# A fused attention and MLP kernel on one core: the channel MLP's first product by seven block products

## Chip, core and metric

The kernel runs on one core of a Trainium2 chip. TensorE multiplies, VectorE (DVE), ScalarE (ACT) and GpSimd (POOL) work on tiles in SBUF and PSUM, and SyncE (SP) issues the DMAs. The metric is the device time of one execution in microseconds.

## What is computed

Four batches of 768 tokens with 8 heads of 48 channels go through a decayed linear attention, and the result (384 channels) through two MLP blocks. The second has a mixing over tokens and one over channels:

```python
# first block: x is the attention's output
xn = (x - mu) / np.sqrt(var + 1e-06) * g_ln
x = x + np.maximum(xn @ w_ch1, 0.0) @ w_ch2           # 384 -> 1536 -> 384
# second block
xt = x.transpose(0, 2, 1)
h = np.maximum(xt @ w_tok1, 0.0) @ w_tok2             # 768 -> 256 -> 768
u = x + h.transpose(0, 2, 1)
h2 = np.maximum(u @ w_ch1, 0.0) @ w_ch2               # 384 -> 1536 -> 384
return u + h2
```

The weights reach the core as pairs of 32-bit integers (the halves of a double).

## The kernel before

Every product is made of three matmuls with operands split in a high and a low part: high by high, high by low, low by high. A weight piece of 128 x 384 is loaded (`sg`, 384 KB), turned into floats by three integer steps on VectorE (`convert`, tile `cu`), and split: the high part by a copy on ScalarE, the low part by a subtraction.

Block 1 does attention, normalization and the first MLP in eight steps of 384 tokens, `m0` to `m7`. In it 32 pieces of the weights of block 2 are converted too (`store`, one every 3.8 units of the schedule): the floats go to HBM (`f_d`), whole and not split. `S7` is the start of the last step, `MP2` that of block 2. In block 1 ScalarE writes the high part of each hidden tile (`hh`), VectorE the low part (`hl`), and only with the latter the PSUM bank comes free; there are three such banks (`mm`).

In the last step of block 1 and the start of block 2, `fetch` loads the 32 pieces again (`wf`, 192 KB) and splits them. The token mixing (`tokmix`) of a batch makes `rt` (the six products `rr`, two banks), its high and low part `rh` and `rl`, the products `hh` (`ht`, six tiles), the sum `uu`, and turns each tile by three transposes (`tp`). The channel MLP (`mlp4`) goes over six tiles of 512 tokens: 12 hidden blocks with 9 matmuls of 512 columns each (`mm1`, tile `mm`), ScalarE's relu, VectorE's `hl`, and output tiles `mo` with 36 matmuls of 384 columns (`mm2`), whose result VectorE adds to `xr` (`fin2`) before the store.

`check` runs beside all this in block 2: for each of the 56 weight pieces a load of 384 KB (`cs`), a square on ScalarE, a comparison on VectorE, a subtraction on POOL and a sum on ScalarE. These are called range steps below; they end in one flag (`okt`).

What sets the order: each engine works in order. Every piece of work has a slot number (`Slots`), one unit being 9 matmuls; the emission is sorted by it, and the first 77 units by a table. SP issues its DMAs in that order as well, and an issue that waits holds back those behind it.

Of the kernel before, what the change touches and what calls it, by code (L numbers as in the profile page):

```python
# [21 lines left out]
C = 128  # L22
# [21 lines left out]
P = dict(A=[7, 10, 16, 22, 30, 38, 46, 54, 62], M0=29, LEAD=7, WS=9, WD=2.2, CS=0.5, JQ=42, JD=3.8, JL=6, CKS=6, CKD=2.45,  # L44
         CHK=148, NV=12, WARM0=56, SG=5, PL=4, J=77)
# [95 lines left out]
@with_exitstack  # L141
def fused_kernel(ctx, tc, q_t, k_t, f_t, v_n, v_t, g_rep, w1, w2, wt1, wt2, w3, w4, out):
    nc = tc.nc
    w1, w2, wt1, wt2, w3, w4 = (w.bitcast(I32) for w in (w1, w2, wt1, wt2, w3, w4))
    w1, w2, w3, w4 = (w.rearrange("p (f c) -> p f c", f=FT) for w in (w1, w2, w3, w4))
    x1_d = tc.dram_tile([NU, C, DM], F32, name="x1_d")
    f_d = tc.dram_tile([32, 128, DM], F32, name="f_d")
    with ExitStack() as main:
        flag = main_path(main, tc, q_t, k_t, f_t, v_n, g_rep, w1, w2, wt1, wt2, w3, w4, out, x1_d, f_d)
    general_path(tc, flag, q_t, k_t, f_t, v_t, g_rep, w1, w2, wt1, wt2, w3, w4, out)  # L150
# [7 lines left out]
def main_path(ctx, tc, q_t, k_t, f_t, v_n, g_rep, w1, w2, wt1, wt2, w3, w4, out, x1_d, f_d):  # L158
# [4 lines left out]
    ap = ctx.enter_context(tc.tile_pool(name="ap", bufs=1))  # L163
    xp = ctx.enter_context(tc.tile_pool(name="xp", bufs=9))
    mmp = ctx.enter_context(tc.tile_pool(name="mmp", bufs=3, space=PSUM))
    scp = ctx.enter_context(tc.tile_pool(name="scp", bufs=2, space=PSUM))
    atp = ctx.enter_context(tc.tile_pool(name="atp", bufs=3, space=PSUM))

    ident = const.tile([128, 128], F32, name="ident")
    upper = const.tile([128, HC], F32, name="upper")  # L170
    gln = const.tile([128, DM], F32, name="gln")
    seg = const.tile([P2, NP, C], F32, name="seg")
# [8 lines left out]
    w1h = wp.tile([128, FT, KT, 128], F32R, name="w1h")  # L181
    w1l = wp.tile([128, FT, KT, 128], F32R, name="w1l")
    w2h = wp.tile([128, FT, DM], F32R, name="w2h")
    w2l = wp.tile([128, FT, DM], F32R, name="w2l")

    xt = ap.tile([128, 36, 128], F32R, name="xt")
# [13 lines left out]
    def convert(s0, ld, src, dones, name, step=1, place=None):  # L200
# [23 lines left out]
        for f, x in zip(dones, "hl"):  # L224
            sl.e(s0 + 3 * step, lambda f=f: f(t["u"]), name + "." + x)

# [6 lines left out]
    at = ExitStack()  # L233
    sg = at.enter_context(tc.tile_pool(name="sg", bufs=P["SG"]))
# [276 lines left out]
    def stands(step):  # L511


        if step < N1:
            i = 18 * (step % 2)
            return [xt[:, j:j + 9].rearrange("p (k u) c -> p k (u c)", k=KT) for j in (i, i + 9)]
        if step % 2 == 0:
            return [xt[:, j:j + 12].rearrange("p (k u) c -> p k (u c)", k=KT) for j in (0, 12)]
        return [h[:, 24:36].rearrange("p (k u) c -> p k (u c)", k=KT) for h in hid2()]

    both = {}

    def hid2():
        if not both:
            both.update((x, hp.tile([128, 36, 128], F32R, tag=x, name=x)) for x in ("hh", "hl"))
        return both["hh"], both["hl"]
# [73 lines left out]
    def mlp4(j, s0, fin, out):  # L600

        t = {}
        step = N1 + j

        def mm1(f):
            ps = t[f] = mmp.tile([128, 512], F32, tag="mm", name="mm")
            ah, al = aT[step]
            i = 0
            for k in range(KT):
                for w, x in ((w1h, ah), (w1h, al), (w1l, ah)):  # L610
                    nc.tensor.matmul(ps, w[:, f, k, :], x[:, k, :], start=(i == 0), stop=(i == 8))  # L611
                    i += 1

        def hid(f):
            return [h[:, 4 * (f % 6):4 * (f % 6) + 4].rearrange("p u c -> p (u c)") for h in hid2()]

        def mm1_h(f):
            nc.scalar.activation(out=hid(f)[0], in_=t[f], func=AF.Relu)  # L618

        def mm1_l(f):  # L620
            hh, hl = hid(f)
            nc.vector.scalar_tensor_tensor(hl, t[f], 0.0, hh.bitcast(F32), op0=ALU.max, op1=ALU.subtract)  # L622

        def mm2(u, g):
            if g % 2 == 0:
                t["o", u] = mmp.tile([128, 512], F32, tag="mm", name="mo")
            ps = t["o", u][:, :DM]
            lo, hi = 6 * (g // 2), 6 * (g // 2) + 5
            for f in range(3 * g, 3 * g + 3):
                a, al = (x[:, 128 * u:128 * u + 128] for x in hid(f))  # L630
                for x, w, i in ((a, w2h, 0), (a, w2l, 1), (al, w2h, 2)):
                    nc.tensor.matmul(ps, x, w[:, f, :], start=(f == lo and i == 0), stop=(f == hi and i == 2))  # L632

        for half in range(2):
            for i in range(6):
                f, q = 6 * half + i, s0 + 14 * half + i
                sl.p(q, lambda f=f: mm1(f))
                sl.e(q + 1, lambda f=f: mm1_h(f))
                sl.late(q + 1, lambda f=f: mm1_l(f))
            for u in range(4):  # L640
                for g in (2 * half, 2 * half + 1):
                    q = s0 + 14 * half + 6 + 2 * u + g % 2
                    sl.p(q, lambda u=u, g=g: mm2(u, g))
                sl.late(q + 1, lambda u=u: fin(u, t["o", u][:, :DM]))
                if half:
                    sl.late(q + 1, lambda u=u: out(u))

# [10 lines left out]

    def fin2(j):
        def f(u, ps):  # L660
            x = us[divmod(4 * j + u, NCH)]
            nc.vector.tensor_tensor(x, ps, x, op=ALU.add)  # L662

        def d(u):
            b, s = divmod(4 * j + u, NCH)
            nc.sync.dma_start(out=out[b, 128 * s:128 * s + 128, :], in_=us.pop((b, s)))
        return f, d

# [21 lines left out]

    def store(i, s0, src, key):

        def out(u):
            kept[key] = f_d[len(kept)]
            nc.sync.dma_start(out=kept[key], in_=u)
        convert(s0, s0 - P["JL"], src, (out,), f"s{i}")

# [30 lines left out]
    jobs = [(w[:, 768 * i:768 * i + 768], (k, i)) for i in range(4) for w, k in ((wt1, "t1"), (wt2, "t2"))]  # L728
    jobs += [(w[:, f], (k, f)) for w, k in ((w3, "w3"), (w4, "w4")) for f in range(FT)]
# [387 lines left out]
```

## Time and profile before

| | |
|---|---|
| median of three runs | 780.83 us (779.58 to 781.37) |
| the profiled execution | 780.75 us |
| its span in the trace | 779.0 us |
| TensorE busy | 768.1 us, 99% |
| VectorE, ScalarE, POOL busy | 408.8, 328.1, 179.8 us |
| granted TensorE clock | 0.998 of full |

Busy shares say which engine works; the chain followed back from the last instruction says which work set the end. An instruction's duration in the trace is longer than its distance from the next of its kind, since matmuls overlap.

### The profile page before, as it was taken

The page shows a single profiled execution, that of the slowest core. Times are in us where ns is not written, and L with a number is a line of the kernel's source. Part 1 is how long each engine was busy: PE and PEld are TensorE (multiplying, and loading weights), DVE is VectorE, ACT ScalarE, POOL GpSimd, SP SyncE. Part 2 cuts the span into 40 slices and gives each one's busy share as a digit, 9 for nine tenths or more (in the row PEclk, how much of TensorE's full clock was granted, in tenths as well). Part 3 has the DMA queues.
Part 4 walks back from the last instruction along what each step waited for, and adds up shares of the span by engine and source line. Part 5 has one row for each costly group of instructions (what it writes and reads, how often), then busy time and mean ns, then how long its engine had stood idle before and what let it go on. Part 6 is the DMA issues. An engine that isn't in the chain of part 4 may idle for free.

```text
span 779.0 us, 16825 instructions
## 1 busy us (share of the span) xinstructions
PE 768.1 (99%) x6966; PEld 719.6 (92%) x6966; DVE 408.8 (52%) x805; ACT 328.1 (42%) x841; POOL 179.8 (23%) x177
## 2 busy tenths in 40 slices
PE   8899999999999999999999999999999999999997
PEld 7789999999999999999999899899899899899886
DVE  7898886575656746454352534434434444334421
ACT  6775463343444434442342534434434434334210
POOL 1344121144224442220023441112011111112000
PEclk9999999999999999999999999999999999999999
DMA  9675252445346453442333633225323343323001
GB/s 268 184 227 162 88 161 76 148 131 162 115 129 179 142 167 108 134 138 66 124 99 112 203 82 96 88 81 158 92 76 102 101 142 88 96 82 113 30 2 45
DMA packets 48613, 93.39 MB, mean 120 GB/s; under 512 B 5520, under 2 KB 26128, under 8 KB 48528
## 3 DMA queue, kind: packets, MB, share of 16 engines
q1 hardware_dynamic: 48528, 92.23, 39.3%
q8 instruction: 56, 0.92, 0.5%
q14 instruction: 29, 0.24, 0.1%
HBM read 76.48 MB, written 15.73 MB: 118 GB/s over the span
## 4 chain that ended last, share of the span: by engine, by line
PE 96%; DMA 2%; DVE 1%; SPq 1%; ACT 0%; issue 0%
PE mo L584 20%; PE mm L554 20%; PE mo L632 19%; PE mm L611 19%; PE rt L793 3%; PE ht L817 3%; PE tp L507 2%; PE yT L393 2%; PE yT L384 2%; DMA first<-in_q_t 2%; PE sc L335 1%; PE sc L347 1%; PE y L436 1%; PE kp L312 1%; SPq L257 0%; PE yT L501 0%
## 5 line engine op out<-in xcount | busy, mean ns | idle before, releaser
L554 PE MATMUL mm<-xt,w1h 128*128 128x384 f32 x576 | 150.4, 342 | 0.0
L554 PEld LDWEIGHTS mm<-xt,w1h 128*128 128x128 f32 x576 | 101.7, 188 | 1.7 <-DVE hl L573 0.2
L584 PE MATMUL mo<-w2h,hh 128*128 128x384 f32 x288 | 101.2, 352 | 0.0
L622 DVE SCALAR_TENSOR_TENSOR hl<-mm,hh 128x512 fp32r<-128x512 f32 x72 | 49.8, 691 | 95.4 <-ACT hh L618 95.4
L870 POOL TENSOR_TENSOR cs<-cs 128x384 f32<-128x384 f32 x56 | 46.5, 831 | 227.0 <-DVE cs L867 166.8
L632 PE MATMUL mo<-w2h,hh 128*128 128x384 f32 x288 | 97.5, 339 | 0.0
L584 PE MATMUL mo<-w2h,hl 128*128 128x384 f32 x288 | 96.6, 335 | 0.0
L554 PE MATMUL mm<-xt,w1l 128*128 128x384 f32 x288 | 96.5, 335 | 0.0
L632 PE MATMUL mo<-w2h,hl 128*128 128x384 f32 x288 | 96.5, 335 | 0.0
L584 PE MATMUL mo<-w2l,hh 128*128 128x384 f32 x288 | 96.4, 335 | 0.0
L632 PE MATMUL mo<-w2l,hh 128*128 128x384 f32 x288 | 96.3, 335 | 0.0
L618 ACT ACTIVATE hh<-mm 128x512 fp32r<-128x512 f32 x72 | 43.1, 598 | 124.9 <-PE mm L611 124.9
L569 ACT ACTIVATE hh<-mm 128x384 fp32r<-128x384 f32 x96 | 46.7, 488 | 85.2 <-PE mm L554 85.1
L573 DVE SCALAR_TENSOR_TENSOR hl<-mm,hh 128x384 fp32r<-128x384 f32 x96 | 52.4, 552 | 40.2 <-ACT hh L569 39.9
L611 PE MATMUL mm<-xt,w1h 128*128 128x512 f32 x216 | 67.2, 392 | 0.0
L662 DVE TENSOR_TENSOR xr<-mo,xr 128x384 f32<-128x384 f32 x48 | 26.7, 556 | 73.1 <-PE mo L632 73.1
L584 PEld LDWEIGHTS mo<-w2h,hh 128*128 128x128 f32 x288 | 54.1, 188 | 1.7
L632 PEld LDWEIGHTS mo<-w2h,hh 128*128 128x128 f32 x288 | 54.1, 188 | 0.5
L632 PEld LDWEIGHTS mo<-w2l,hh 128*128 128x128 f32 x288 | 54.1, 188 | 0.4
L584 PEld LDWEIGHTS mo<-w2l,hh 128*128 128x128 f32 x288 | 54.2, 188 | 0.0
L554 PEld LDWEIGHTS mm<-xt,w1l 128*128 128x128 f32 x288 | 54.1, 188 | 0.0
L632 PEld LDWEIGHTS mo<-w2h,hl 128*128 128x128 f32 x288 | 54.1, 188 | 0.0
(162 smaller groups left out, 1486.9 us busy)
## 6 DMA issues: line engine op xcount, KB each, us to landing
cs<-in_w SPq DMA_DIRECT2D x48, 384.0 KB, 3.2
sg<-in_w SPq DMA_DIRECT2D x44, 384.0 KB, 4.6
f_d<-cu SPq DMA_DIRECT2D x32, 192.0 KB, 2.8
wf<-f_d SPq DMA_DIRECT2D x32, 192.0 KB, 2.6
F<-in_f_t SPq DMA_DIRECT2D x21, 224.0 KB, 3.2
T<-in_k_t SPq DMA_DIRECT2D x21, 224.0 KB, 3.1
T<-in_q_t SPq DMA_DIRECT2D x21, 224.0 KB, 4.0
x_d<-x SPq DMA_DIRECT2D x24, 192.0 KB, 2.0
```

Source lines behind the costliest of these rows:

```text
L554: nc.tensor.matmul(ps, w[:, f, k, :], x[:, k, :], start=(i == 0), stop=(i == 8))
L569: nc.scalar.activation(out=hid(f)[0], in_=t[f], func=AF.Relu)
L573: nc.vector.scalar_tensor_tensor(hl, t[f], 0.0, hh.bitcast(F32), op0=ALU.max, op1=ALU.subtract)
L584: nc.tensor.matmul(ps, x, w[:, f, :], start=(f == lo and i == 0), stop=(f == hi and i == 2))
L611: nc.tensor.matmul(ps, w[:, f, k, :], x[:, k, :], start=(i == 0), stop=(i == 8))
L618: nc.scalar.activation(out=hid(f)[0], in_=t[f], func=AF.Relu)
L622: nc.vector.scalar_tensor_tensor(hl, t[f], 0.0, hh.bitcast(F32), op0=ALU.max, op1=ALU.subtract)
L632: nc.tensor.matmul(ps, x, w[:, f, :], start=(f == lo and i == 0), stop=(f == hi and i == 2))
L662: nc.vector.tensor_tensor(x, ps, x, op=ALU.add)
L793: nc.tensor.matmul(t["r"][j][:, :DM], w[:, s, js], t[x, s], start=(s == 0 and i == 0), stop=(s == NCH - 1 and i == 2))
L817: nc.tensor.matmul(ps[:, :DM], w[:, j, js], x[:, j], start=(i == 0), stop=(i == 5))
L870: nc.gpsimd.tensor_tensor(t["u"], t["u"], t["h"], op=ALU.subtract)
```

## The change

The first product of the channel MLP, u by w_ch1, takes a batch's tokens in two halves (three tiles each, 384 columns), and the hidden channels in two halves as well (block f and block f+6). The sum over 384 channels has three blocks. In `strassen` seven products (1, 2, 6, 7, 5, 3, 4), of 11 block pairs in all, replace 12 block pairs of 384 columns. A group `G(g)`, g = 0 to 5, makes hidden blocks g and g+6 for the 768 tokens. Operands are ten sums of token blocks (`xsh`, `xsl`) and nine sums of weight blocks (`ws`, high in 0 to 8 and low in 9 to 17). Product 1 has a bank of its own (`ex`), the others stand in pairs of banks (`pp`, two pairs). VectorE forms the results of a group by four additions (`add2`, two in `add3`, `add4`), three of them 768 columns wide, ScalarE copies product 1 (`copy1`) and takes the high parts (`hi`); the low parts are a 768-column step each (`lo`), on VectorE or POOL.

The weight sums are formed in block 1: a pair of pieces of w_ch1 needs four 128-column sums on VectorE. All 32 pieces are split there and kept in HBM as two parts (`f_d`, `h_d`, `t_d`). In block 2 they are loaded ready: six loads of 1.18 MB (`weights3`), eight of 0.59 MB (`weights4`), and the token weights by 256 KB for every use (`ts`, two buffers). Token mixing of the next batch stands in the groups: RR 0 within group 0, and so on; it has `rt` in two of the three single banks. `check` starts later and its steps come every 3.2 units instead of 2.45, with two buffers for three.

```diff
-P = dict(A=[7, 10, 16, 22, 30, 38, 46, 54, 62], M0=29, LEAD=7, WS=9, WD=2.2, CS=0.5, JQ=42, JD=3.8, JL=6, CKS=6, CKD=2.45,
-         CHK=148, NV=12, WARM0=56, SG=5, PL=4, J=77)
+P = dict(A=[7, 10, 16, 22, 30, 38, 46, 54, 62], M0=29, LEAD=7, WS=9, WD=2.2, CS=0.5, JQ=42, JD=3.8, JL=6, CKS=16, CKD=3.2, CKL=3.2,
+         CHK=199, NV=12, WARM0=56, SG=5, PL=4, J=77)
...
+        def cut(h, l, x, le=nc.vector):
+            nc.scalar.activation(out=h, in_=x, func=AF.Copy)
+            le.tensor_tensor(l, x, h.bitcast(F32), op=ALU.subtract)
...
+            if i == 0:
+                e.scalar_tensor_tensor(v[:, 0], b[:, 0], -1.0, b[:, 1], op0=ALU.mult, op1=ALU.subtract)
+                e.tensor_tensor(v[:, 2], a[:, 0], b[:, 0], op=ALU.subtract)
+            elif i == 1:
+                e.scalar_tensor_tensor(v[:, 1], v[:, 0], -1.0, a[:, 0], op0=ALU.mult, op1=ALU.subtract)
+                e.tensor_tensor(v[:, 3], a[:, 1], v[:, 1], op=ALU.subtract)
+            elif i == 2:
+                cut(r[:, 4:6], q[:, 4:6], b[:, 1:3])
+            else:
+                cut(r[:, 0:4], q[:, 0:4], v[:, 0:4], nc.gpsimd)
...
+    def load_t(m, s):
+        t = tsp.tile([128, 2, JT, 128], F32R, tag="ts", name="ts")
...
+    for g in range(6):
+        sl.e(S7 + FT + 2 + .5 * g, lambda g=g: weights3(g))
+    for i, f in enumerate((0, 6, 3, 9)):
+        sl.e(MP2 + (10, 11, 16, 18)[i], lambda f=f: weights4(f, 3))
...
+        mix = {1: ((6, 5),), 2: ((7, 6), (8, 7)), 6: ((1, 3),), 7: ((2, 2), (5, 9)), 5: ((0, 0),), 3: ((3, 8), (8, 9)),
+               4: ((4, 4), (5, 1))}
+        place = {2: (26, 0), 6: (26, 1), 7: (75, 0), 5: (75, 1), 3: (34, 1), 4: (34, 0)}
...
+            ops = [(w, x) for i, j in mix[m] for w, x in ((ws[:, g, i], xsh[:, j]), (ws[:, g, i], xsl[:, j]),
+                                                          (ws[:, g, 9 + i], xsh[:, j]))]
...
+            nc.scalar.activation(out=q[:, 1], in_=t.pop((g, 1)), func=AF.Copy)
...
+            nc.vector.tensor_tensor(q[:, 0:3:2], t.pop((g, 26))[:, :, :DM], q[:, 1:2].to_broadcast([128, 2, DM]), op=ALU.add)
...
+            nc.vector.tensor_tensor(u, t[g, 75][:, :, :DM], q[:, 2:3].to_broadcast([128, 2, DM]), op=ALU.add)
+            nc.vector.tensor_tensor(q[:, 1], t.pop((g, 75))[:, 1, :DM], u[:, 0], op=ALU.add)
...
+            nc.vector.tensor_tensor(u, t.pop((g, 34))[:, :, :DM], u, op=ALU.add)
...
+        plan = [(G, 0, [0]), (RR, 1), (G, 1, [2]), (RR, 3), (RR, 4), (G, 2, [5]), (RE, 0), (O, 0, 0, E), (O, 1, 0, E),
+                (O, 0, 0, [2]), (O, 1, 0, [2]), (O, 2, 0, R3), (HH, 0), (HH, 3), (O, 3, 0, R3), (HH, 1), (HH, 4),
+                (O, 4, 0, R3), (HH, 2), (HH, 5), (O, 5, 0, R3),
+                (G, 3), (G, 4), (G, 5), (O, 0, 1, E), (TR, 0), (O, 1, 1, E), (TR, 1),
+                (O, 0, 1, [2]), (O, 1, 1, [2]), (TR, 2), (O, 2, 1, R3), (O, 3, 1, R3), (O, 4, 1, R3), (O, 5, 1, R3)]
...
-    cp = ctx.enter_context(tc.tile_pool(name="cp", bufs=3))
+    cp = ctx.enter_context(tc.tile_pool(name="cp", bufs=2))
```

In the plan O(u, half, groups) is the second product of output tile u, RE the split of `rt`, HH and TR the token mixing's second product and the transposes.

**Place A.** VectorE in step `m3` of block 1, before (`hl` frees a bank of the first MLP, `cu` is a conversion, `xn` the normalization):

```order
L573 SCALAR_TENSOR_TENSOR hl<-mm,hh 128x384
L217 SCALAR_TENSOR_TENSOR cu<-sg,cu 128x384
L454 SCALAR_TENSOR_TENSOR xn<-y,nm,gln 128x384
L573 SCALAR_TENSOR_TENSOR hl<-mm,hh 128x384 x2
L207 TENSOR_SCALAR cu<-sg 128x384
L573 SCALAR_TENSOR_TENSOR hl<-mm,hh 128x384
L212 SCALAR_TENSOR_TENSOR cu<-sg,cu 128x384
L573 SCALAR_TENSOR_TENSOR hl<-mm,hh 128x384
```

The same place after (the `sg` steps of 128 and 256 columns are sums and the subtraction of a pair):

```order
L565 SCALAR_TENSOR_TENSOR hl<-mm,hh 128x384
L213 SCALAR_TENSOR_TENSOR cu<-sg,cu 128x384
L457 SCALAR_TENSOR_TENSOR xn<-y,nm,gln 128x384
L565 SCALAR_TENSOR_TENSOR hl<-mm,hh 128x384
L657 SCALAR_TENSOR_TENSOR sg<-cu 128x128
L658 TENSOR_TENSOR sg<-cu 128x128
L565 SCALAR_TENSOR_TENSOR hl<-mm,hh 128x384
L203 TENSOR_SCALAR cu<-sg 128x384
L660 SCALAR_TENSOR_TENSOR sg<-sg,cu 128x128
L661 TENSOR_TENSOR sg<-cu,sg 128x128
L565 SCALAR_TENSOR_TENSOR hl<-mm,hh 128x384
```

Two sums come ahead of the second `hl` of the former pair, and two more ahead of the next.

**Place B.** VectorE in block 2 before, where the token product `rt` of the third batch is split:

```order
L867 SCALAR_TENSOR_TENSOR cs<-cs 128x384
L622 SCALAR_TENSOR_TENSOR hl<-mm,hh 128x512 x2
L867 SCALAR_TENSOR_TENSOR cs<-cs 128x384
L807 SCALAR_TENSOR_TENSOR rl<-rt,rh 128x384 x2
L622 SCALAR_TENSOR_TENSOR hl<-mm,hh 128x512
```

And after, in group 2 of a batch and at the turn to the second product (`q`, `u` are the additions, `hl` the low parts):

```order
L902 TENSOR_TENSOR q<-mm,q 128x2x384
L907 TENSOR_TENSOR u<-mm,q 128x768
L908 TENSOR_TENSOR q<-mm,u 128x384
L1092 SCALAR_TENSOR_TENSOR cs<-cs 128x384
L912 TENSOR_TENSOR u<-mm,u 128x768
L934 SCALAR_TENSOR_TENSOR hl<-q,hh 128x768
L822 SCALAR_TENSOR_TENSOR rl<-rt,rh 128x384 x2
L934 SCALAR_TENSOR_TENSOR hl<-u,hh 128x768
```

The split `rl` stands behind an addition and a low part of 768 columns each, and the last `hl` behind it.

**Place C.** SP around the start of block 2, before (`wf` are weight pieces, `xr` tokens, `cs` range loads):

```order
L860 DMA cs<-in_w 128x768
L758 DMA wf<-f_d 128x384
L777 DMA xr<-x_d 128x384
L758 DMA wf<-f_d 128x384
L777 DMA xr<-x_d 128x384
L860 DMA cs<-in_w 128x768
L758 DMA wf<-f_d 128x384 x2
```

And after (`ts` are the token weights, `w2h` and `w2l` the second weights):

```order
L792 DMA xr<-x_d 128x384
L767 DMA ts<-t_d 128x512
L792 DMA xr<-x_d 128x384
L767 DMA ts<-t_d 128x512
L777 DMA w2h<-h_d 128x1152
L777 DMA w2l<-h_d 128x1152
L777 DMA w2h<-h_d 128x1152
L777 DMA w2l<-h_d 128x1152
L1085 DMA cs<-in_w 128x768
L777 DMA w2h<-h_d 128x1152
```

The large loads stand behind the token loads of the next batch, and the last of these waits for a buffer that RR 3 of the batch frees; the range load comes behind the first four.

## Rows read from the trace of the kernel before

**Rows 1.** The page: busy time of the engines, and the chain's shares.

```profile
PE 768.1 (99%) x6966; PEld 719.6 (92%) x6966; DVE 408.8 (52%) x805; ACT 328.1 (42%) x841; POOL 179.8 (23%) x177
PE 96%; DMA 2%; DVE 1%; SPq 1%; ACT 0%; issue 0%
```

**Rows 2.** Busy time by stretch: us, engines, clock, DMA share, GB/s.

```profile
118.00:379.00 261.00, 261.00 (x3167) 250.54 (x3167) 147.52 (x302) 104.03 (x263) 72.37 (x57) 1.00 0.41 127
...
430.80:774.00 343.20, 342.59 (x1784) 314.80 (x1782) 139.38 (x249) 131.24 (x353) 59.86 (x69) 1.00 0.32 94
```

**Rows 3.** The chain of work that ended last: start, us, what.

```profile
421.07 0.33 PE tp L507 x3
...
723.67 12.28 PE mm L611 x54
...
760.88 12.52 PE mo L632 x72
```

**Rows 4.** Groups of the page: line, names, shapes, count, busy us, mean ns.

```profile
L632 PE MATMUL mo<-w2h,hh 128*128 128x384 f32 x288 | 97.5, 339 | 0.0
...
L611 PE MATMUL mm<-xt,w1h 128*128 128x512 f32 x216 | 67.2, 392 | 0.0
```

**Rows 5.** TensorE's timeline around three transposes: start, us, engine, line.

```profile
420.90 0.49 PE L507 MATMUL tp<-ident,xr 128*128 128x128 f32 x3
421.15 0.42 PE L584 MATMUL mo<-w2h,hh 128*128 128x384 f32 x1
421.41 0.34 PE L584 MATMUL mo<-w2l,hh 128*128 128x384 f32 x1
```

**Rows 6.** Groups by shape, blocks 1 and 2: durations of VectorE's steps.

```profile
L573 DVE SCALAR_TENSOR_TENSOR hl<-mm,hh 128x384 fp32r<-128x384 f32 x96 | 52.4, 552 | 40.2 <-ACT hh L569 39.9
...
L622 DVE SCALAR_TENSOR_TENSOR hl<-mm,hh 128x512 fp32r<-128x512 f32 x72 | 49.8, 691 | 95.4 <-ACT hh L618 95.4
...
L867 DVE SCALAR_TENSOR_TENSOR cs<-cs 128x384 f32<-128x384 f32 x56 | 31.6, 565 | 0.3 <-issue 0.3
...
L807 DVE SCALAR_TENSOR_TENSOR rl<-rt,rh 128x384 fp32r<-128x384 f32 x6 | 3.1, 551 | 0.5 <-ACT rh L801 0.5
```

**Rows 7.** Timeline of the end: the last matmul, the addition, the store.

```profile
773.05 0.34 PE L632 MATMUL mo<-w2h,hl 128*128 128x384 f32 x1
773.42 0.56 DVE L662 TENSOR_TENSOR xr<-mo,xr 128x384 f32<-128x384 f32 x1 [2.57 <-PE mo L632]
774.01 0.33 SPq L666 DMA_DIRECT2D out<-xr  x1
```

**Rows 8.** Timeline in step m3: VectorE, and TensorE's weight load (PEld).

```profile
159.24 1.00 DVE L573 SCALAR_TENSOR_TENSOR hl<-mm,hh 128x384 fp32r<-128x384 f32 x2
159.84 0.30 PEld L554 LDWEIGHTS mm<-xt,w1h 128*128 128x128 f32 x2 [0.21 <-DVE hl L573]
160.44 0.54 DVE L573 SCALAR_TENSOR_TENSOR hl<-mm,hh 128x384 fp32r<-128x384 f32 x1
...
162.24 0.56 DVE L573 SCALAR_TENSOR_TENSOR hl<-mm,hh 128x384 fp32r<-128x384 f32 x1 [0.79 <-ACT hh L569]
...
163.80 0.56 DVE L573 SCALAR_TENSOR_TENSOR hl<-mm,hh 128x384 fp32r<-128x384 f32 x1 [0.54 <-ACT hh L569]
```

**Rows 9.** DMA issues of the page: names, count, KB each, median us to landing.

```profile
wf<-f_d SPq DMA_DIRECT2D x32, 192.0 KB, 2.6
F<-in_f_t SPq DMA_DIRECT2D x21, 224.0 KB, 3.2
T<-in_k_t SPq DMA_DIRECT2D x21, 224.0 KB, 3.1
```

**Rows 10.** DMA of two stretches with full queues, 11 to 12 and 13 to 15 us.

```profile
DMA packets 189, 0.28 MB, mean 282 GB/s; under 512 B 24, under 2 KB 158, under 8 KB 189
...
DMA packets 310, 0.81 MB, mean 404 GB/s; under 512 B 34, under 2 KB 60, under 8 KB 310
```

More of the change, by code (lines that the diff above doesn't have):

```diff
@@ L511, in stands @@
     def stands(step):
[L514 to L526, printed above, removed]
+        i = 18 * (step % 2)
+        return [xt[:, j:j + 9].rearrange("p (k u) c -> p k (u c)", k=KT) for j in (i, i + 9)]
     def transposed(step, u, ps):
@@ L598, in mlp @@
             sl.late(q + 1, lambda u=u: out(u), f"{m}d{u}")
[L600 to L646, printed above, removed]
     def fin1(step):
@@ new lines, in main_path, with hid2, pair @@
+    exp = ctx.enter_context(tc.tile_pool(name="exp", bufs=1, space=PSUM))
+    xsh = p2.tile([128, 10, 384], F32R, name="xsh")
+    xsl = p2.tile([128, 10, 384], F32R, name="xsl")
+    hids = []
+    def hid2():
+        if not hids:
+            hids.extend(hp.tile([128, 36, 128], F32R, tag=x, name=x).rearrange("p (f u) c -> p f (u c)", f=FT)
+                        for x in ("hh", "hl"))
+        return hids
+    def pair(name):
+        return ppp.tile([128, 2, 512], F32, tag="pp", name=name)
@@ L790, in rr, with lt @@
+            t[s] = x[:, 0], x[:, 1]
+            split(t[s][0], t[s][1], us[b, s], nc.vector)
+        def lt(m, s):
+            t["w", m, s] = load_t(m, s)
+        def rr(s):
+            w0 = t.pop(("w", 0, s))
+            if s == 0 and b:
+                t["r"] = [bank("rt")[:, :DM] for _ in range(JT)]
+            elif s == 0:
+                ps = pair("rt")
+                t["r"] = [ps[:, j, :DM] for j in range(JT)]
             for j in range(JT):
-                js = slice(128 * j, 128 * j + 128)
@@ new lines, in main_path, with xmix, mixed @@
+    QA, QD, QP, QS = 0.32, 0.36, 0.55, 0.13
+    def xmix(T, i, end, free=0):
+        sl.e(end + QS, lambda: T["xc"](i))
+        sl.e(end + QS + .6, lambda: T["xs_s"](i))
+        sl.e(max(end + QS + 1.1, free), lambda: T["xs_p"](i))
+    def mixed(T, s, end):
+        sl.e(end + QS, lambda: T["uu"](s))
+    T0 = tokmix(0)
+    for s in range(NCH):
+        sl.e(S7 + 1 + .4 * s, lambda s=s: T0["ld"](s))
+        sl.e(S7 + 1 + .4 * s, lambda s=s: T0["lt"](0, s))
+        sl.e(S7 + 2.5 + .8 * s, lambda s=s: T0["sp"](s))
+        sl.p(S7 + 4 + .9 * s, lambda s=s: T0["rr"](s))
@@ L853, in check @@
+    end = MP2 + 1
+    for b in range(B):
+        end = double(b, end)
+    cp = ctx.enter_context(tc.tile_pool(name="cp", bufs=2))
     def check(i, s0, src):
@@ L873, in fifth @@
             nc.scalar.activation(out=t["u"], in_=t["u"], func=AF.Abs, accum_out=wlow[:, i:i + 1])
-        for d, f in ((-4, first), (0, second), (1, third), (2, fourth), (4, fifth)):
+        for d, f in ((-P["CKL"], first), (0, second), (.6, third), (1.2, fourth), (2.2, fifth)):
             sl.e(s0 + d, f)
@@ L908, in main_path @@
     sl.e(MP2 + P["CHK"] + 2, ranges_e)
-    sl.run(MP2 + 28 * 6 + 2)
+    sl.run(end + 3)
     flag = nc.values_load(oki[0:1, 0:1], min_val=0, max_val=1)
```

367 lines of the change are left out of this document (266 added, 101 removed).

## The prediction

> **What bounds the kernel now.** I read the engines' busy shares and the chain of work that ended last first. TensorE is busy 99% of the span and is 96% of the chain [rows 1]; the second MLP, where the change acts, holds 343.2 us of which TensorE works 342.59 [rows 2]. So the kernel takes what TensorE's instructions take, one behind the other. An instruction's own duration misleads, since they overlap; the chain gives the pitch. 54 first products of 512 columns took 12.28 us, 227.4 ns each; 72 second products of 384 columns took 12.52 us, 173.9 ns each [rows 3]. VectorE's load is the second thing to read: 147.52 of 261.0 us (57%) in block 1, 139.38 of 343.2 (41%) in block 2 [rows 2]. It has room, but as an average.
>
> **What the change takes from TensorE.** Before, the first product of the second MLP is 648 instructions of 512 columns (the 216 of [rows 4], and four forms of 108): 648 x 227.4 ns = 147.4 us. After, a group is 11 block pairs (seven products, four of them of two pairs), three instructions each, 384 columns wide; six groups per batch, four batches: 6 x 4 x 33 = 792 instructions. Those have the shape of the second product, so 792 x 173.9 ns = 137.7 us. Gain: 9.7 us. Transposes: 24 groups of three become 12 groups of six. The next matmul starts 0.25 us after a group of three began, and its successor 0.26 us later instead of 0.17 [rows 5], so each break costs some 0.09 us beside the transposes; the chain's 0.33 us for such a group [rows 3] says the same. 12 breaks fewer are 1.0 us by that and 0.8 if the breaks cost less behind six; I take 0.8. Second product, token mixing and attention keep their instructions. Against the profiled execution (span 779.0 us, 1.75 us around it, 780.75 in all, 0.08 below the median of 780.83) TensorE alone would give 780.75 - 10.5 = 770.25 us. The rest is what TensorE will now wait for.
>
> **VectorE in a group: tight, mostly covered.** Sums of pairs of banks (768 columns) don't occur before. An addition from PSUM of 512 columns takes 691 ns and of 384 takes 552 [rows 6], 139 ns for 128 more, so by a straight line 768 take 0.97 us (0.70, if wide reads cost only what 512 do, to 1.11, two of 384). A group asks add2 0.97, add3 0.97 + 0.56, add4 0.97, lo 0.97: 4.4 us, with a part of a range step (0.565, one per some 5 us) 5.0, of 33 x 0.174 = 5.74. VectorE reads a finished product some 0.2 us after its slot [rows 7]. With a group's start at 0, product 6 ends at 2.09, so add2 runs from 2.29 to 3.26, and the bank pair is wanted at 3.65; add3 ends at 5.38, wanted at 6.26; add4 runs 5.94 to 6.91, wanted at 7.83. Margins of 0.39, 0.88 and 0.92 us: no stall in the plain case, and one range step in front of add2 uses up the first. TensorE's end is set by it only where VectorE falls behind. I charge nothing here; the price if the cover goes is a rival.
>
> **The turn from the first to the second product (three times).** Behind group 2, VectorE has add4 (`u`), lo (`hl`), then the two splits `rl` of the token product and the last `hl` in a row (place B of the order). The token product's banks come free only with `rl`, and the second output tile needs one. add4 ends at 0.2 + 0.97 = 1.17 us from the end of the group, lo at 2.14, the first rl (0.55 us, [rows 6]) at 2.69; TensorE arrives there after 12 second products, 2.09 us. Wait: 0.6 us at each of two turns, 1.3 us (0 to 2.7, with a range step in between). The turn of the first batch is counted below.
>
> **Block 1: more VectorE work between steps that TensorE waits for.** 26 of the 32 weight pieces get a subtraction of about 0.55 us there, the other six (each the second of a pair) four 128-column sums (0.27 us each on the line above) and a 256-column subtraction (0.42): 14.3 + 9.0 = 23 us, which makes 57% about 66. The place matters: at place A of the order the pair's steps come between the subtractions `hl` that free the banks of the first MLP. Before, the weight load of the product that starts at 159.84 us already waited 0.21 us for `hl`, and VectorE runs on without a gap until 160.98 [rows 8]. In after, 0.55 us come ahead of the next `hl` and 0.55 more ahead of the one behind it; idle gaps of 0.79 and 0.54 us follow [rows 8]. I estimate 0.3 us per pair, 1.7 us for six (0, if the gaps take all; 4.5 at 0.75 each).
>
> **The last step of block 1 and the first batch: loads.** Weights for the token mixing come by 256 KB loads into two buffers. In the last step two of them are issued when their buffer comes free, only 15 matmuls (2.6 us) ahead of their use. 192 KB took 2.6 us and 224 KB 3.1 to 3.2 [rows 9]; I take 2.9, so 0.3 us each, 0.6 (0 to 1.5). In batches 0 to 2 one load (for the RR before the last) has 18 matmuls, 3.13 us, the same way: 0 to 0.3 each, 0.5 in all. The six loads of the first weights (1.18 MB each) are issued from about 31 us into the last step; RR of the next batch needs the token data queued behind them at 55.9 us. With full queues the microsecond from 11 moved 282 GB/s, 158 of its 189 packets under 2 KB; the two from 13 moved 404, with 60 of 310 so small [rows 10]. At 404, 7.08 MB are through at 48.5 us and nothing waits; at 282 they are through at 55.9, the token data with 1.6 us of transfer and 2 of landing at 59.5: 3.6 us. I take 404, since the new loads are of long rows (9216 bytes per partition). The second weights' loads stand on SP behind a token load that waits for the end of RR 3 (place C). From there to the first second product are 45 matmuls, 7.8 us; the four loads wanted are 2.36 MB: 5.8 us at 404 and some 2 us to land, with issues 8.3, so 0.5 us late; at 282 GB/s 3.1. In the same turn a range step stands on ScalarE ahead of `rh` and on VectorE ahead of `rl`; it waits for its own load, behind the weights, so the bank wait that is 0.6 elsewhere becomes about 2.2 us. First batch: 0 + 0.5 + 2.2 = 2.7 us (1 to 8.9).
>
> Row against rule: the stretch from 13 us moved 404 GB/s [rows 10]. The Trainium skill, DMA: Bandwidth & Descriptors, section "Specifications", puts the limit from HBM for one core at about 358 GB/s. The trace exceeds it for two whole microseconds, so I don't use it; by it (an estimate) the second weights would take 6.6 us instead of 5.8 and the sum would rise by 0.8 us.
>
> **End.** The flag's bank and the range steps now close inside the last groups: 0.5 us (0 to 1). The path behind the last product stays: the final addition of 384 columns and its store [rows 7].
>
> **Sum.** 1.3 + 1.7 + 0.6 + 0.5 + 2.7 + 0.5 = 7.3 us of waits against a gain of 10.5: 770.25 + 7.3 = 777.55, say 777.5 us.
>
> **Rivals.**
> (a) Hidden after all: the gaps of block 1 take the added work, the loads run at 404 GB/s, the range step's load lands early, and `rl` costs nothing because wide reads are cheaper than the line. Waits of at most 3 us: 771 to 773, say 772. For it: TensorE had no wait worth naming in block 2 before [rows 2], and the margins in a group are positive. Against it: the turn has a wait by durations that are measured.
> (b) Slower: VectorE falls behind in the groups. It works in order, so one step that waits (a range step or a token split whose load or ScalarE partner is late) or is priced too low delays add2, the pair of product 3 then comes late, and the lag is passed on to the next group, since 5.0 of 5.74 us leave little to recover. It decides from a lag of 0.45 us per group on: 24 x 0.45 = 10.8 us alone take the gain. With 2.5 us of the other terms 770.25 + 10.8 + 2.5 = 783.5. For it: the first margin, 0.39 us, is less than one range step of 0.565 [rows 6], and groups 0 to 2 hold six token splits of about 0.55 us each too. Against it: the plain sum, 4.4 us, leaves 1.3.
> (c) No change: the loads at the start of block 2 run at 310 GB/s, between the rows. The first weights are then through at 53.6 us, the token data at 57.1, 1.2 us late; the second weights take 7.6 + 2.5 us against 7.8, 2.3 us late instead of 0.5: 777.5 + 3.0 = 780.5. At 282 it is 3.6 + 2.6 more, 783.7. For it: stores, token loads and range loads share the queues, and 282 was measured with them full; against it: small packets made that number [rows 10].
>
> **How the numbers follow.** Forecast with its surroundings (775 to 779.3) 0.45, of which 0.03 lie within 0.2% of before; (a) 0.20; (c) 0.15; (b) 0.20. 0.2% of the time is 1.56 us, about what a measurement of this kernel tells from no change: faster is below 779.27, slower above 782.39. Faster 0.42 + 0.20 = 0.62, within 0.18, slower 0.20. The range takes in most of (a) and half of (b): 771.5 to 784.
>
> **What would show it.** The chain must show groups of 33 matmuls with 5.74 us, 792 in all at 173.9 ns; if the pitch is larger the first term falls. TensorE's idle time should stand at the turn behind every third group of the first half, with `rl` as releaser; in block 1 behind `hl` where pairs are summed; around the start of block 2 behind loads. TensorE idle in front of product 3 or 2 in most groups, released by the additions, means (b). Range steps waiting for their loads at the start of block 2, and weights landing over 8 us after their issue, mean (c). No idle time at the turns means (a). A 768-column addition of 1.2 us or more would make the forecast wrong upward; below 0.8 us, downward.

## The result and the profile after

The changed kernel takes 789.38 us (median of 4 runs, 789.25 to 793.19) against 781.1 us of before: 1.0122 of its time, interval 1.0089 to 1.0155. It is slower by 8 to 9 us, and lies 5 us above the range of the prediction. One execution of a later run (928 us, at a granted clock of 0.752) belongs to a slow state and is left out of all comparisons. The profiled execution has 789.25 us and a span of 787.5 us. The page's engine totals and the chain's shares, to be put beside [rows 1]:

```profile
PE 763.5 (97%) x7110; PEld 734.8 (93%) x7110; DVE 525.8 (67%) x969; ACT 367.8 (47%) x899; POOL 195.5 (25%) x175
PE 73%; DVE 8%; DMA 5%; issue 5%; ACT 4%; POOL 2%; SPq 1%; DVEq 0%; POOLq 0%; ACTq 0%
```

TensorE works less, as meant, but it no longer is the whole chain: 27% of it now runs over other engines, DMAs and issues. The stretches that answer to [rows 2] (us, busy time of PE, PEld, DVE, ACT, POOL, clock, DMA share, GB/s):

```profile
118.00:379.00 261.00, 260.41 (x3161) 249.53 (x3154) 178.75 (x357) 120.30 (x300) 82.02 (x63) 1.00 0.50 160
432.00:785.50 353.50, 337.36 (x1928) 330.33 (x1926) 222.57 (x348) 157.88 (x381) 78.53 (x72) 1.00 0.40 127
```

In block 1 VectorE has 31 us more work (23 were forecast), and TensorE loses next to nothing. In block 2 TensorE stands still for 16 of 353.5 us; it was 0.6 of 343.2. The chain's rows that answer to [rows 3] (start, us, what), and VectorE's additions by shape, which answer to [rows 6]:

```profile
485.42 15.10 PE mm L892 x87
...
763.25 18.74 PE mo L945 x108
```

```profile
L912 DVE TENSOR_TENSOR u<-mm,u 128x768 f32<-128x768 f32 x24 | 23.0, 957 | 7.5 <-PE mm L892 6.9
L902 DVE TENSOR_TENSOR q<-mm,q 128x768 f32<-128x768 f32 x24 | 22.9, 955 | 10.2 <-ACT cs L1089 4.8 <-PE mm L892 4.6 <-ACT q L898 0.7
```

The pitch of the new products is 15.10 / 87 = 173.6 ns (173.9 forecast), a 768-column addition 0.955 us (0.97 forecast). What the forecast did not have stands in TensorE's waits from 420 us on (what waited, for what: us, times, longest):

```profile
PE mm L892 <- DVE q L902: 4.1, 5, 2.3
PE rt L812 <- DVE xx L763: 2.1, 3, 1.0
PE mo L945 <- DMA w2l<-h_d: 1.8, 1, 1.8
PE mo L945 <- DVE xr L949: 1.3, 2, 0.9
PE mo L945 <- DVE rl L822: 1.2, 3, 0.6
PE okt L1125 <- DVE ok L1121: 1.2, 1, 1.2
```

A wait shown here is shorter than what it costs, since the weight load ahead of a matmul is late too. So I took the distances between the starts of neighbouring matmuls and subtracted the usual pitch of the first one's shape; what the matmul behind a wait loses is counted with the wait. In block 2 the excess is 20.3 us after and 3.2 us before. These 17.1 us, the 1.1 us by which block 2 begins later, and the gain of 9.7 us by the pitches give 8.5 us, the difference of the spans (787.5 and 779.0). The 1.1 us are uncertain: in the traces of the experiments on the changed kernel, whose block 1 is the same, block 2 begins anywhere from 430.5 to 433.6 us. The large pieces after: 5.0 us at the first turn from first to second product (456 to 462 us), 5.4 us in five groups, ahead of products 3 or 2 (`q`), 3.5 us in five token products (`xx`, the split of the token data), 2.0 us for output banks (`xr`), 1.1 us at the other two turns (`rl`), 1.5 us for the flag (`okt`), 0.5 us at one second token product.

Two places show what the engines wait for. At the longest wait for `q`, VectorE and ScalarE (start, us, engine, and in brackets the idle time ahead with its releaser):

```profile
621.46 0.56 DVE L1092 SCALAR_TENSOR_TENSOR cs<-cs 128x384 f32<-128x384 f32 x1 [2.98 <-ACT cs L1089]
621.94 0.95 DVE L902 TENSOR_TENSOR q<-mm,q 128x768 f32<-128x768 f32 x1
```

```profile
620.74 0.54 ACT L1089 ACTIVATE cs<-cs 128x384 f32<-128x384 f32 x1 [2.48 <-DMA cs<-in_w]
```

VectorE stands idle for 2.98 us with the addition `q` ready behind a range step (`cs`); that one waits for its square on ScalarE, and the square for its load. The load was late for a reason on SP, seen in the chain of this stretch:

```profile
612.95 0.48 DVE xr L949
...
613.45 0.33 SPq L952
...
613.82 1.50 SPq L792
...
615.90 4.74 DMA cs<-in_w
```

A store of the batch just finished waited for its addition, the token load came behind it, and only then the range load was issued. The second place is ScalarE in a group, at 541.78 us: the last sum of a range step waits for POOL's subtraction, with `hh`, the relu, and the split of the next token data behind it; VectorE then waits 1.92 us for that split. The split itself lasts 1.88 us instead of 0.55, while POOL forms a low part, and add2 (`q`) comes late:

```profile
541.78 0.56 ACT L1098 ACTIVATE cs<-cs 128x384 f32<-128x384 f32 x1 [1.00 <-POOL cs L1095]
542.33 0.83 ACT L924 ACTIVATE hh<-u 128x768 fp32r<-128x768 f32 x1
543.20 0.85 ACT L927 ACTIVATE u<-u 128x768 f32<-128x768 f32 x1
543.95 0.51 ACT L762 ACTIVATE xx<-xr 128x384 fp32r<-128x384 f32 x1
...
544.12 1.83 POOL L932 TENSOR_TENSOR hl<-u,hh 128x768 fp32r<-128x768 f32 x1 [2.38 <-ACT u L927]
...
544.49 1.88 DVE L763 TENSOR_TENSOR xx<-xr,xx 128x384 fp32r<-128x384 f32 x1 [1.92 <-ACT xx L762]
```

ScalarE's waits for POOL over block 2, before and after (us, times, longest):

```profile
ACT cs L873 <- POOL cs L870: 8.2, 8, 2.1
```

```profile
ACT cs L1098 <- POOL cs L1095: 67.4, 36, 5.7
```

So the theory after the result was R: the 56 range steps, which the kernel before has too, now stand in the way on three engines and in SP's queue. Its rival W: the wide additions overfill VectorE by themselves.

### The profile page after: what moved, and what is told of

The parts are those of the page before. It is cut to its first block, busy times and chain, and to the rows that moved or that the text cites. A ratio compares the mean times of both kernels' runs of the same rounds, so it can differ in the third digit from the quotient of the medians.

```text
span 787.5 us, 17589 instructions
## 1 busy us (share of the span) xinstructions
PE 763.5 (97%) x7110; PEld 734.8 (93%) x7110; DVE 525.8 (67%) x969; ACT 367.8 (47%) x899; POOL 195.5 (25%) x175
## 4 chain that ended last, share of the span: by engine, by line
PE 73%; DVE 8%; DMA 5%; issue 5%; ACT 4%; POOL 2%; SPq 1%; DVEq 0%; POOLq 0%; ACTq 0%
PE mo L576 19%; PE mm L546 17%; PE mm L892 11%; PE mo L945 11%; DMA cs<-in_w 3%; PE ht L834 3%; PE yT L396 2%; PE rt L812 2%; PE yT L387 2%; PE sc L338 2%; DMA first<-in_q_t 2%; PE sc L350 1%; PE y L439 1%; POOL cs L1095 1%; PE tp L510 1%
## 5 line engine op out<-in xcount | busy, mean ns | idle before, releaser
L546 PE MATMUL mm<-wx 128*128 128x384 f32 x864 | 163.2, 340 | 0.4 <-DVE hl L565 0.4
L546 PEld LDWEIGHTS mm<-wx 128*128 128x128 f32 x864 | 148.5, 188 | 2.5 <-DVE hl L565 1.1
L892 PE MATMUL mm<-xsh,wx 128*128 128x384 f32 x528 | 139.0, 335 | 4.1 <-DVE q L902 4.1
L892 PEld LDWEIGHTS mm<-xsh,wx 128*128 128x128 f32 x528 | 95.8, 188 | 5.7 <-DVE q L902 5.7
L1095 POOL TENSOR_TENSOR cs<-cs 128x384 f32<-128x384 f32 x56 | 49.0, 876 | 207.1 <-DVE cs L1092 171.6
L892 PE MATMUL mm<-xsl,wx 128*128 128x384 f32 x264 | 88.2, 334 | 0.0
L1098 ACT ACTIVATE cs<-cs 128x384 f32<-128x384 f32 x56 | 31.0, 554 | 67.4 <-POOL cs L1095 67.4
L945 PEld LDWEIGHTS mo<-w2h,hh 128*128 128x128 f32 x288 | 54.4, 189 | 5.3 <-DVE rl L822 2.4
L945 PEld LDWEIGHTS mo<-w2h,hl 128*128 128x128 f32 x288 | 54.5, 189 | 0.0
L576 PEld LDWEIGHTS mo<-w2h,hl 128*128 128x128 f32 x288 | 54.0, 188 | 0.0
```

The source lines that it names most:

```text
L892: nc.tensor.matmul(ps, w, x, start=n == 0, stop=n == len(ops) - 1)
L945: nc.tensor.matmul(ps, x, w[:, f], start=(g % 3 == 0 and m == 0 and n == 0), stop=(g % 3 == 2 and m == 1 and n == 2))
L1095: nc.gpsimd.tensor_tensor(t["u"], t["u"], t["h"], op=ALU.subtract)
L1098: nc.scalar.activation(out=t["u"], in_=t["u"], func=AF.Abs, accum_out=wlow[:, i:i + 1])
```

## Experiments

Each is compared with the kernel before in the same session (medians 780.0 to 781.4 us). Where a run is set against the changed kernel ("after"), that is its 789.38 us.

**Range steps left out**, of the changed kernel and of the one before. Neither checks the range of the weights.

```diff
-    for i, src in enumerate(pieces):
-        check(i, MP2 + P["CKS"] + P["CKD"] * i, src)
+    sl.e(MP2 + 1.1, lambda: nc.vector.memset(wsum, 0.0))
+    sl.e(MP2 + 1.1, lambda: nc.vector.memset(wlow, 0.0))
```

> The changed kernel without its 56 range steps (no load, square, comparison, subtraction or sum of them; the flag's sums are set to zero). Theory R (range steps standing in ScalarE's, VectorE's and SP's order cause most of the new waits): of the 17 us that TensorE waits more in block 2 at least 10 go, 789.4 becomes 777 or less, and the 2.5 us wait of a group for its first addition is gone. Theory W (the 768-column additions and low parts alone overfill VectorE in the groups): less than 4 us go, 785 or more, and waits for add2 stay in most groups.

> The kernel before without its 56 range steps. Both theories: TensorE bound it with only 3 us of excess in block 2, so no change beyond 0.2%: 779.5 to 782. If it gets faster by 3 us or more, range steps cost the kernel before as well, and what e1 gains is not the change's.

Measured: after without them 774.85 us (ratio to before 0.9923, 0.9898 to 0.9948), before without them 780.06 (1.000, 0.998 to 1.002). So the range steps cost the changed kernel 14.5 us and the kernel before nothing that can be told. All of TensorE's waits for `q`, `xx` and `xr` are gone; those left from 420 us on are

```profile
PE mo L945 <- DMA w2l<-h_d: 2.0, 1, 2.0
PE okt L1125 <- DVE ok L1121: 1.3, 1, 1.3
PE mo L945 <- DVE rl L822: 0.6, 2, 0.3
```

W falls: without range steps no group waits.

**Loads or work.** The range steps' work stays, on two tiles in place; their 56 loads are left out.

```diff
-            s = cp.tile([128, 384, 2], I32, tag="cs", name="cs")
-            nc.sync.dma_start(out=s.rearrange("p n t -> p (n t)"), in_=src)
+            s = still[i % 2]
```

> The changed kernel with all range steps' work on ScalarE, VectorE and POOL, but on two tiles that stay in place: the 56 loads are left out. If the late loads are what holds ScalarE and VectorE, the result comes within 2 us of the run without any range steps (about 777). If the time of the steps themselves in the engines' order is what costs, it stays within 2 us of 789.

Measured: 782.26 us (1.001, 0.999 to 1.003), between the two forecasts: of the 14.5 us the loads make 7.1 and the work 7.4. Late loads are half of it.

**The old distances of a range step's parts**, on top of that:

```diff
-        for d, f in ((-P["CKL"], first), (0, second), (.6, third), (1.2, fourth), (2.2, fifth)):
+        for d, f in ((-P["CKL"], first), (0, second), (1, third), (2, fourth), (4, fifth)):
```

> As the run with range steps on tiles in place (no loads), but the steps behind the square at 1, 2 and 4 units, as in the kernel before, instead of 0.6, 1.2 and 2.2. There ScalarE waited 73.6 us for POOL's subtraction, with copies and splits queued behind; in the kernel before 8.2 us. If these waits in ScalarE's order make what the steps themselves cost, 782.3 falls to 775 to 778. If it is the engines' sheer time, it stays at 781 or more.

Measured: 778.1 us (0.998, 0.996 to 0.999). 4.2 of the 7.4 us come back with the same work, by distance alone; ScalarE's waits for POOL fell from 73.6 (33 times) to 54.4 us (22 times). The time is at the upper edge of what was expected, and 3.3 us stay that distance doesn't explain. The traces say the same of block 2 alone (from the first product of the first group to the end): 355.6 us after, 348.0 without the loads, 344.2 with the old distances on top, 341.3 without range steps.

**The second weights earlier.**

```diff
-        sl.e(MP2 + (10, 11, 16, 18)[i], lambda f=f: weights4(f, 3))
+        sl.e(MP2 + (1.2, 4, 16, 18)[i], lambda f=f: weights4(f, 3))
```

> The changed kernel with the first four loads of the second weights issued at 1.2 and 4 units after the start of block 2 instead of 10 and 11, ahead of token loads that wait for RR. By the trace the first turn from first to second product lost 5.1 us (0.6 + 2.1 for the loads, 1.4 at half clock behind them, 1.0 for rl behind a range load of 9.6 us). If the SP order causes it, 3.5 to 5 us go: 784 to 786. If the loads only collide with token loads, the wait moves to RR and less than 1 us goes.

Measured: 786.07 us (1.006, 1.004 to 1.009), 3.3 us less than after; TensorE's waits for `w2h` and `w2l` are gone, and the wait for `rl` at that turn stays (0.9 us in the distances). SP's order made them; the gain is just short of the expected 3.5 us.

**Range steps moved, first way**: all work kept, none in groups 0 to 2 and none in a batch's last 3 units, evenly spread over the rest.

```diff
-        check(i, MP2 + P["CKS"] + P["CKD"] * i, src)
+        d = room * (i + .5) / len(pieces)
+        for a, b in calm:
+            if d < b - a:
+                break
+            d -= b - a
+        check(i, a + d, src)
```

> The changed kernel with all of its work; only the 56 range steps are moved: none in groups 0 to 2 of a batch and none in the last 3 units of a batch (where stores and token loads stand on SP), a little denser elsewhere. Theory of the range steps in the way: the waits for add2 and for the token splits, 8.9 us in the trace of after, go for the most part, and 789.4 becomes 780 to 783. If any denser place costs the same, it stays above 786.

Measured: 783.75 us (1.004, 1.003 to 1.005), just outside: 5.6 us less. The place isn't all that changed: a range load is also issued closer to its square, 2.6 units ahead instead of 3.2. The waits for token splits are gone, but groups 3 to 5 now wait for `q`, and second products for `xr` behind the sums of the transposed tokens. Together with early weights, `rh` and `rl` directly behind RR 5, the flag's transpose later, and no range step among the transposes (the parts of a range step are also closer together here, 0.55, 1 and 1.8 units behind the square, and the load 2.4 ahead):

```diff
                     for s in then:
                         cur = RR(s)
+                        if s == NCH - 1:
+                            RE(0)
...
-    sl.p(MP2 + P["CHK"] + 1, ranges_t)
+    sl.p(MP2 + P["CHK"] + 3, ranges_t)
```

> All work kept: range steps outside groups 0 to 2, the transposes and a batch's end; the second weights' first loads early; rh and rl directly behind the last RR, inside group 2, ahead of products 3 and 4; the flag's transpose 3 units behind its sums instead of 1. By the waits seen in the traces: 789.4 less 8.9 (groups and token splits), 4 (loads), 1.1 (rl), 2 (output banks behind transposes), 1.4 (flag) gives 772; 771 to 776 expected, faster than both kernels. If the range steps only move the waits, 780 or more.

Measured: 779.45 us (0.999, 0.997 to 1.001): a miss. The waits at the turns, for `xr` and for the flag are gone; what stays are 6.8 us in seven groups; in most of them a range step stands ahead of add2 or add3 on VectorE, having waited up to 2.3 us for its square, as in the line below. How much of this the closer parts make isn't shown.

```profile
571.13 0.56 DVE L1102 SCALAR_TENSOR_TENSOR cs<-cs 128x384 f32<-128x384 f32 x1 [2.31 <-ACT cs L1099]
```

To see that nothing else was hidden under them, the same three moves (early weights, early `rh` and `rl`, later flag) without any range step:

> The changed kernel without range steps, with the second weights' loads early, rh and rl inside group 2 and the flag's transpose later. What is left should be TensorE's instructions and little else: 774.85 less 2.3, 0.9 and 1.4 gives 770.3 (769 to 772), which is the gain of 10.5 us that the count of matmuls and transposes gives. If the count is wrong or VectorE still holds the groups, 773 or more.

Measured: 771.58 us (0.988, 0.985 to 0.990). TensorE has one wait left in block 2:

```profile
PE rt L812 <- DVE xx L763: 0.6, 1, 0.6
```

**Range steps in phase with the groups.** One per group, its comparison between add3 and add4, its square ahead of the first high part, its last sum behind the relu; the others among second products, none among transposes; the three moves as above.

```diff
             q = at(max(e[5], q), .97, "add3")
+            t3 = q + .01
...
+            if b or g:
+                times.append((t3 - 4.2, t3 - .9, t3, t3 + .4, r + .2))
...
+            if step in ((O, 0, 0, E), (O, 2, 1, R3)):
+                n, gap = (6 if T else 4, 2.35) if step[2] == 0 else (3 if T else 0, 2.4)
+                at0 = cur + (1.8 if step[2] == 0 else .6)
+                times.extend((x - 3.2, x, x + .6, x + 1.2, x + 2.2) for x in (at0 + gap * k for k in range(n)))
```

> All work kept, with the second weights' loads early and rh, rl inside group 2 as in the combined run, but the range steps stand in phase with the groups: one per group, its comparison between add3 and add4, its square ahead of the first high part, its last sum behind the relu; the others stand among the second products, none among the transposes. The combined run still waited 7.3 us, nearly all in groups where a range step stood ahead of an addition. If the place within the group is what counts, these go: 771 to 775. If each group with a range step loses about 1 us wherever it stands, 778 or more.

Measured: 774.31 us (0.991, 0.988 to 0.993), with all of the work, and faster than both kernels. VectorE in a group, from the trace of the last variant below, which has the same groups:

```profile
579.60 0.56 DVE L908 TENSOR_TENSOR q<-mm,u 128x384 f32<-128x384 f32 x1
580.07 0.55 DVE L1105 SCALAR_TENSOR_TENSOR cs<-cs 128x384 f32<-128x384 f32 x1
580.68 0.96 DVE L912 TENSOR_TENSOR u<-mm,u 128x768 f32<-128x768 f32 x1
581.56 0.95 DVE L934 SCALAR_TENSOR_TENSOR hl<-q,hh 128x768 fp32r<-128x768 f32 x1
582.84 0.96 DVE L902 TENSOR_TENSOR q<-mm,q 128x768 f32<-128x768 f32 x1 [0.33 <-PE mm L892]
```

And in the run without range steps, the same place:

```profile
579.53 0.56 DVE L908 TENSOR_TENSOR q<-mm,u 128x384 f32<-128x384 f32 x1
580.56 0.96 DVE L912 TENSOR_TENSOR u<-mm,u 128x768 f32<-128x768 f32 x1 [0.47 <-PE mm L892]
```

VectorE has a gap of 0.47 us ahead of add4, where product 4 is not done yet, and the 0.55 us of the comparison fill it; add2 still waits 0.33 us for TensorE. The move changes distances too: in a group the comparison now stands 0.9 units behind the square and the last sum about 3 (0.6 and 2.2 in after), so place and distance aren't separated by it. The phase alone, without early weights and early `rl`:

> The changed kernel with the range steps in phase with the groups (and the flag later) and nothing else moved. Against e9 it lacks the early weight loads and the early rl: by the waits seen, 2.3 + 1.0 (half clock) + 2 us over e9, so 776 to 780 if the place within the group is what counts; 783 or more, as with the first way of moving them, if not.

Measured: 777.1 us (median of six; 0.994, 0.992 to 0.996), 12.3 us less than after, by the place of the range steps within the groups, their distances and the later flag. What the early weights and the early `rl` add isn't shown: the medians lie 2.8 us apart, but the intervals overlap, and the profiled executions are alike (774.05 us here, 774.57 with them). With them the waits for the second weights and for `rl` are gone, but the first HH waits 2.3 us for a token load, and TensorE's clock is then granted at half its rate for some 3 us.

**The last loads of the second weights later.** This starts from the run in phase with the three moves, where the first HH waited 2.3 us for a token load behind these loads on SP.

```diff
-        sl.e(MP2 + (1.2, 4, 16, 18)[i], lambda f=f: weights4(f, 3))
+        sl.e(MP2 + (1.2, 4, 27, 29)[i], lambda f=f: weights4(f, 3))
```

> As the run with range steps in phase and three other moves, but the last four loads of the second weights, which are wanted only in the second half of the batch, at 27 and 29 units instead of 16 and 18. There a token load issued behind two of them came 2.3 us late for the first HH. If the order on SP made that wait, 774.3 becomes 771.5 to 773; if another load takes their place, it stays.

Measured: 772.76 us (0.989, 0.987 to 0.992), the fastest with all of the work, 16.6 us below after and 8 below before. The wait of the first HH is gone; the step from 774.31 us isn't clear of the noise, since the intervals overlap. TensorE's waits from 420 us on, and ScalarE's for POOL:

```profile
PE rt L812 <- DMA ts<-t_d: 0.5, 1, 0.5
PE rt L812 <- DVE xx L763: 0.5, 1, 0.5
PE mm L892 <- DVE q L902: 0.4, 1, 0.4
```

```profile
ACT cs L1111 <- POOL cs L1108: 55.8, 30, 3.0
```

ScalarE still waits 55.8 us for POOL, while TensorE's waits come to 1.4 us in all: what counts is who is queued behind such a wait.

**POOL's low parts on VectorE**, tried on the changed kernel, since all of VectorE's stretched steps overlapped a step of POOL.

```diff
-                at(r + QS, 1.06, "lo", 1, nc.gpsimd)
+                at(h1 + QS, .6, "lo", 1, nc.vector)
```

> The changed kernel with all 16 low parts of POOL (768 columns, 1.85 us each) on VectorE, behind the other low part of the group; nothing else moved. In the trace of after 15 steps of VectorE with operands in SBUF last longer than usual (11.3 us in all, up to 1.88 us for 0.55), and each overlaps a step of POOL. If POOL's low parts cause this and with it the waits for token splits, VectorE's stretched steps fall to those that meet POOL's range subtraction (8 or fewer, 4 us), ScalarE waits less for POOL, and the time falls to 784 to 787 although VectorE gets 15 us more. If the stretched steps are only idle time in another guise, VectorE's 15 us more make the groups later: 792 or more.

Measured: 788.87 us (1.011, 1.008 to 1.015), the time of after. The contention of VectorE and POOL is shown: 8 stretched steps with 4.6 us are left, all of them beside POOL's range subtraction, and the waits in token products fall from 3.5 to 0.7 us. The time follows neither forecast. TensorE waits for `q` in five groups nearly as long as before (3.4 us in its list, 4.1 in after), and the first turn costs nearly 2 us more: the wait for the weights is 0.5 us instead of 2.7, but the one for `rl` 3.4 instead of 1.1, behind a range step whose square waited 3.89 us for its load, and the half clock behind it lasts twice as long. So this run doesn't tell what the contention by itself is worth. The stretch at half clock (clock 0.50, third number from the end), and ScalarE's wait for POOL:

```profile
459.60:466.20 6.60, 5.96 (x19) 5.96 (x20) 1.91 (x4) 1.45 (x5) 0.80 (x1) 0.50 0.79 311
```

```profile
ACT cs L1098 <- POOL cs L1095: 68.3, 35, 6.3
```

So POOL's low part is not what makes that wait; POOL itself waits for the comparison on VectorE (171.6 us in block 2 of after).

## Why the prediction was wrong

- **The gain, right.** 10.5 us forecast. In the run without range steps and with the three moves, block 2 from the first product of the first group to the end takes 338.0 us, and 348.3 before: 10.3 us. The 0.97 us for a wide addition held too (0.955), though the 691 and 552 ns it was drawn from are low parts (`hl`), not additions.
- **Block 1 and its last step, right in kind, too large.** 1.7 + 0.6 us forecast; the first group starts at 431.89 us, and the first product of before at 430.77: 1.1 us, with the scatter named above. In block 1 TensorE waited for `hl` behind one pair of the six, 0.4 and 0.2 us at 208 and 213 us, where two steps of the pair took 1.40 and 1.47 us instead of 0.29 and 0.42, each beside a step of POOL; at the others it didn't wait, though VectorE had 31 us more work and not 23. The 0.5 us for token weights within the batches didn't come: no wait for `ts` stands in the list.
- **The turns, right.** 0.6 us at each of the later two; 1.1 us for both in the distances, and `rl` as releaser. (The sum has 1.3 for twice 0.6.)
- **The first batch, mechanism right, too small.** 2.7 us forecast (0.5 for the weights, 2.2 for `rl` behind the range step), 5.0 measured: 0.6 + 2.1 us for the weights, 1.1 for `rl`, 1.2 for half clock. The first weights came without a wait, as forecast, at 404 and 407 GB/s over 8 us each. While the second came, from 450 to 458 us, the core moved 352 GB/s: between the rows, as rival (c) had it, and (c)'s price for them, 2.3 us, is near the 2.7 measured. But without range steps it moved 398 GB/s there, and the last weight was still 2.0 us late, so the wait does not need the lower rate. The stretches of after, and the last one without range steps:

```profile
412.00:420.00 8.00, 8.00 (x50) 7.89 (x49) 2.55 (x6) 0.87 (x2) 0.00 (x0) 1.00 1.00 404
420.00:428.00 8.00, 8.00 (x52) 7.93 (x51) 6.13 (x17) 4.66 (x11) 0.00 (x0) 1.00 1.01 407
450.00:458.00 8.00, 6.42 (x36) 5.84 (x34) 5.04 (x5) 1.00 (x2) 1.28 (x1) 1.00 0.97 352
```

```profile
450.00:458.00 8.00, 6.53 (x38) 6.21 (x36) 6.40 (x7) 2.98 (x6) 1.66 (x1) 1.00 1.02 398
```

  In both runs the loads for the second half of the batch, which the sum had left out, were queued right behind the four. That they took part of the rate is the likely reason; no run tests it alone.

  The Trainium skill, DMA: Bandwidth & Descriptors, section "Specifications", gives about 358 GB/s as the limit from HBM for one core; the measurement decides against it here.
- **The end, too small.** 0.5 us forecast, 1.5 measured.
- **The step that failed: "VectorE in a group ... I charge nothing here".** Its sum was right (add2 0.955 us, and no group waits without range steps). The failure is that the margin was worked out for VectorE alone. For the first turn the sum did look at the order on ScalarE and SP (place C); for the groups, the token products and the output banks it went through none but VectorE's, though the diff shows two buffers for three and shorter distances between a range step's parts. At 616 us a store and a token load ahead of it on SP made a range load late; elsewhere, with the last sum 2.2 units behind the square instead of 4, ScalarE arrived there ahead of POOL and waited, 36 times in 56. Both waits hold copies and splits for which VectorE, and then TensorE, waits. In the distances that was 5.4 + 3.5 + 2.0 + 0.5 = 11.4 us, where the sum had zero. With the 2.8 us by which the first turn is longer than without range steps (5.0 against 2.2), that is nearly the 14.5 us of the run without them.
- **Rival (b) named the mechanism** ("one step that waits ... delays add2") and its side, with 783.5 us and a chance of 0.20. Its form was wrong: not 0.45 us in each of 24 groups, but 0.2 to 2.6 us in five groups, five token products and four other places. It came on top of the other terms. The view of ScalarE's waits would have raised its chance: before, ScalarE already waited 8.2 us for POOL (8 times) with 4 units from the square to the last sum, and the diff cuts them to 2.2.

What stays open: how the 7.1 us of the loads divide between SP's order and the number of buffers (a third buffer wasn't tried), and how the gain of the run in phase divides between the place of a step and the distances of its parts.

## To carry to other kernels

Side work that costs nothing while one engine bounds the kernel is free only by its margins; when a change takes work from that engine, cost every in-order queue that the side work passes, with what stands behind each of its waits, and not the busy shares. Place such steps in phase with the main loop, in a gap that the trace shows (here 0.47 us ahead of add4), instead of at an even distance that meets the loop at every phase: the same work cost 14.5 us one way, and 2.3 to 2.7 us the other (777.1 against 774.85 us without it, and with the other moves 774.31 against 771.58). The run in phase also sets a step's parts further apart, which by itself gave 4.2 us. A total of waiting time on a side engine says little: ScalarE's 67 us for POOL came with 17 us of waits on TensorE, 56 us with nearly none.

## What the runs showed of the hardware

In block 2 of after 15 steps of VectorE with two operands in SBUF were stretched, by 11.3 us in all. Each met a step of POOL under way and ended 0.15 to 0.8 us behind it; before it was 6 steps with 2.75 us. The additions that read PSUM were not stretched. The other way round, POOL's range subtraction, 0.83 us as a rule, took 0.94 to 1.48 us where it began within such a step of VectorE. The Trainium skill, SBUF — State Buffer, section "SBUF: two separate sides", says that such a VectorE step and a GpSimd step hold a shared pair of ports by turns, each for the whole instruction; the trace agrees.

Behind the wait for the second weights, TensorE's clock was granted at half its rate for 3.4 us. TensorE had waited 0.45 us, issued one matmul and waited 1.84 us; the matmuls behind it stand 0.32 us apart instead of 0.174. The stretch of the fall, and two of those matmuls:

```profile
458.30:461.70 3.40, 2.93 (x8) 2.42 (x8) 1.38 (x3) 2.06 (x5) 0.74 (x1) 0.50 1.02 414
```

```profile
459.51 0.52 PE L945 MATMUL mo<-w2h,hh 128*128 128x384 f32 x1
459.83 0.52 PE L945 MATMUL mo<-w2l,hh 128*128 128x384 f32 x1
```

That is 1.2 instead of 2.4 GHz, and it cost about 1.2 us. In the run without range steps one wait of 2.0 us stands at the same place, in the run with the phase alone one of 0.8 and one of 1.5 us with a matmul between, and in both the clock stays full. So a wait of this length may or may not be followed by such a fall.
